# Wider loads of q, k and v, and output steps ahead of gate steps, in an attention and gated feed-forward kernel

## Chip, cores and metric

One core of one Trainium2 chip. The metric is the device time of one execution in microseconds (us). A time is the median of several executions, and each kernel was timed in turns with the kernel before on the same chip.

## The reference

Condensed:

```python
def _attn_ref(q, k, v):                      # (8, 12, 448, 64) each
    scores = np.matmul(q, k.transpose(0, 1, 3, 2)) / np.sqrt(q.shape[-1])
    attn = np.exp(scores - np.max(scores, axis=-1, keepdims=True))
    attn = attn / (np.sum(attn, axis=-1, keepdims=True) + 1e-09)
    return np.matmul(attn, v)

def _moe_ref(x, w_gate, w_val, w_out):       # x (3584, 768), d_ff 1536
    g = x @ w_gate
    return (g / (1 + np.exp(-g)) * (x @ w_val)) @ w_out
# ... x is the attention's output, heads side by side
```

## The kernel before

The 96 heads are worked in 48 pairs. One list of "visits" interleaves three score chunks of attention (matmul, then exponential) with products (sums, probabilities times values) and with steps of the feed-forward: a gate step with its value step for one block of d_ff, or an output step. GpSimd issues the loads of q, k and v, which cast from 32 to 16 bits, and it also arranges q and k for a transpose that is done by DMA. It does that for pair `pr + 3`, and loads for pair `pr + 6`, when the scores of pair `pr` begin.

```python
def load_qk16(pr, n=2):
    h0 = 2 * (pr % 2) if pr >= 14 else 0
    if h0 == 0:
        # ... a new buffer for two pairs: q16, k16 (five in turn)
    for dst, src in ((q16, q), (k16, k)):
        # ... flat: the 2 * n heads
        if pr >= SPLIT:                      # pairs from 12
            split_load(dst, h0, flat, src is q)   # two issues: partitions 0-63, 64-127
            continue
        # ...

# in each visit, after the scores:
for pr in entered:                           # pairs whose first chunk is in this visit
    if pr >= SPLIT:
        double_rest(pr)                      # GpSimd: a copy inside v
    if NPE <= pr + 3 < NPAIR:
        prep(pr + 3)                         # GpSimd: 4 copies; SyncE: DMA transpose
    if 14 <= pr + LA < NPAIR:
        load_qk16(pr + LA, 1)                # LA = 6
    if 4 <= pr // GP + 1 < NGRP:             # GP = 3
        r = pr % GP
        load_v(pr // GP + 1, 2 * r, 2 * r + 2)
# ... products ...
for pr in entered:
    for w in wq.pop(pr, []):                 # weights: {..., 6: V 3, o 0; 7: o 1}
        emit(w)
# ... blocks 2 and later; nf and no are the numbers of gate and of output steps
for y in range(nf):
    if fvq:
        run_fv()
for _ in range(no):
    run_o()
```

The softmax here doesn't subtract the row's maximum and nothing guards it: scores larger than these inputs give would overflow.

Of the kernel before, what the change touches and what calls it, by code (L numbers as in the profile page):

```python
# [11 lines left out]
FP16 = mybir.dt.float16  # L12
# [6 lines left out]
GP = 3  # L19
NPE = 11  # L20
LA = 6
RB = 5
# [3 lines left out]
SPLIT = 12  # L26
# [3 lines left out]
def kernel(  # L30
# [10 lines left out]
    nc = tc.nc  # L41
    B, H, S, D = q.shape
    DM = H * D
    DF = moe_w_gate.shape[1]
    P = 112
    NC = S // P
# [3 lines left out]
    NPAIR = B * NHP  # L50
    NGRP = NPAIR // GP
# [22 lines left out]
    raws = ctx.enter_context(tc.tile_pool(name="raws", bufs=2))  # L74
# [38 lines left out]
            nc.sync.dma_start(dst[:], src[0, 2 * pr : 2 * pr + 2].rearrange("h (p c) d -> p h (c d)", c=NC))  # L113
        raw[pr] = (rq[:], rk[:])

    pairbuf = []

    def load_qk16(pr, n=2):
        h0 = 2 * (pr % 2) if pr >= 14 else 0
        if h0 == 0:  # L120
            rows = 128 if pr >= SPLIT else P
            q16 = raws.tile([rows, 4, NC, D], FP16, tag="rq", bufs=RB, name="q16")
            k16 = raws.tile([rows, 4, NC, D], FP16, tag="rk", bufs=RB, name="k16")
            pairbuf[:] = [q16, k16]
        q16, k16 = pairbuf
        for dst, src in ((q16, q), (k16, k)):
            flat = src.rearrange("b h s d -> (b h) s d")[2 * pr : 2 * pr + 2 * n]
            if pr >= SPLIT:
                split_load(dst, h0, flat, src is q)
                continue  # L130
            nc.gpsimd.dma_start(dst[:, ds(h0, 2 * n)], flat.rearrange("h (p c) d -> p h (c d)", c=NC))
        for i in range(n):
            h = h0 + 2 * i
            raw[pr + i] = (q16[:, h : h + 2], k16[:, h : h + 2])

    def split_load(dst, h0, flat, query):
        n = flat.shape[0]
        by7 = flat.rearrange("h (r x) d -> r h x d", x=7)
        lo = (0, 3) if query else (0, 4)
        at = (0, 0) if query else (0, 1)  # L140
        for u, (x0, x1) in enumerate((lo, (lo[1], 7))):
            nc.gpsimd.dma_start(  # L142
                dst[ts(u, RS), h0 : h0 + n, at[u] : at[u] + x1 - x0, :].rearrange("p h c d -> p h (c d)"),
                by7[:, :, x0:x1, :].rearrange("r h x d -> r h (x d)"),
            )

    def load_v(g, lo=0, hi=2 * GP):
        b = g // GPB
        h0 = (g % GPB) * 2 * GP
        split = b * NHP >= SPLIT  # L150
        if lo == 0:
            v16[g] = raws.tile([128 if split else P, 2 * GP, NC, D], FP16, tag="vt", bufs=3, name="vt")
        if split:
            split_load(v16[g], lo, v[b, h0 + lo : h0 + hi], False)
            return
        nc.gpsimd.dma_start(
            v16[g][:, lo:hi],
            v[b, h0 + lo : h0 + hi].rearrange("h (p c) d -> p h (c d)", c=NC),
        )

    def double_rest(pr):
        g, r = divmod(pr, GP)
        nc.gpsimd.tensor_copy(v16[g][RS:128, 2 * r : 2 * r + 2, 0], v16[g][0:RS, 2 * r : 2 * r + 2, 0])
# [123 lines left out]
    def pv_rest(p0):  # L287
        acc = [ps_f.tile([128, 512], FP32, tag="f", name="acc") for _ in range(2)]
        for t in range(2):
            for j in range(4):  # L290
                g, r = divmod(p0 + j // 2, GP)
                for half in range(2):
                    rows = ts(half, RS)
                    nc.tensor.matmul(  # L294
                        acc[half][ts(j, 32), ds(t * H2, H2)],
                        lhsT=v16[g][rows, 2 * r + j % 2, 0, :].rearrange("p (d t) -> p t d", t=2)[:, t],
                        rhs=E[p0 + 1][rows, 3, j % 2, ds(j // 2 * H2, H2)],
                        start=(t == 0),
                        stop=False,
                    )  # L300
        return acc
# [48 lines left out]
    def scaled(p0, t, acc):  # L350
        b, hp = divmod(p0, NHP)
        kk, bb = divmod(b, NB)
        if kk not in X:
            X[kk] = xp.tile([128, NCB, NB * S], FP16, tag="X", name="X")
        nc.vector.tensor_tensor(  # L355
            X[kk][:, hp + t, ts(bb, S)], acc[:, 0:S], R[p0][:], ALU.mult
        )
# [147 lines left out]
    with tc.manual_schedule():  # L505
# [27 lines left out]
        def emit(item):  # L533
            if item[0] == "qk":
                load_qk16(*item[1:])
            elif item[0] == "V":
                load_v(item[1])
            else:
                load_w(*item)
# [4 lines left out]
        def pop_deferred(n=1):  # L544
            for _ in range(n):
                if deferred:
                    deferred.pop(0)()
# [5 lines left out]
        def add_block(i, visits):  # L553
            f1, f2, n = block(i)
            oq.extend(ffn2_wait)
            ffn2_wait.clear()
            fvq.extend([(f1, NCB * n / 2400.0)] * NFB)
            own = [(f2, NFB * OH / 2400.0)] * (2 * (n // 128))
            (oq if i == 0 else ffn2_wait).extend(own)
            count.update(visits=visits, fv=NFB, o=len(oq), at=0, more=NFB - visits)  # L560
# [8 lines left out]
        def run_o():  # L569
            gen, t = oq.pop(0)  # L570
            next(gen)
            pop_deferred(2)
            return t
# [6 lines left out]
        def left():  # L580
            return sum(2 * t for _, t in fvq) + sum(t for _, t in oq)
# [51 lines left out]
        while g < len(units) or queue:  # L633
            n = 2 if g < (WIDE - FIRST) * NC else 3
# [12 lines left out]
        def product(kind, p0):  # L647
            if kind == "sums":
                pop_deferred(99)
                deferred.extend(recips(p0, sums(p0)))  # L650
            elif kind == "both":
                pop_deferred(99)
                pv_split(p0, rests.pop(p0))
            else:
                if kind == 0:
                    pop_deferred(99)
                scaled(p0, kind, pv(p0, kind))

        def score(pr, c):
            if c == "rest":  # L660
                qk_rest(pr)
            elif pr >= SPLIT:
                qk_split(pr, c)
            else:
                qk(pr, c)
# [4 lines left out]
        for x, (chunks, todo) in enumerate(plan):  # L670
            for pr, c in chunks:
                score(pr, c)
            for _, kind, p0 in todo:
                if kind == "both":
                    rests[p0] = pv_rest(p0)
            end = min([y for y in adds if y > x] + [len(plan) + 1])
            if x == 0:
                for t in range(2):
                    scaled(p4, t, halves[t])
                add_block(0, end)  # L680
            turn2 = None
            entered = [pr for pr, c in chunks if c == 0]
            for pr in entered:
                if pr >= SPLIT:
                    double_rest(pr)
                if NPE <= pr + 3 < NPAIR:
                    prep(pr + 3)
                if 14 <= pr + LA < NPAIR:
                    load_qk16(pr + LA, 1)
                if 4 <= pr // GP + 1 < NGRP:  # L690
                    r = pr % GP
                    load_v(pr // GP + 1, 2 * r, 2 * r + 2)
            for pr, c in chunks:
                if c == 2 and pr < NPE - 2:
                    prep(pr + 2)()
            any_p = len(todo)
            if x in adds and x > 0:
                while todo:
                    product(*todo.pop(0)[1:])
                add_block(adds[x], end - x)  # L700
            while todo:
                product(*todo.pop(0)[1:])
            for pr in entered:
                for w in wq.pop(pr, []):
                    emit(w)
            tiled[0] = bool(any_p) and (not chunks or chunks[0][0] >= TILED)
            if adds[max(y for y in adds if y <= x)] < 2:
                carry = run_budget(left() / (end - x) + carry)
            else:
                at, n = count["at"], count["visits"]  # L710
                no = share(count["o"], at, n)
                nf = 1
                if no and count["more"] > 0:
                    o_left = sum(1 for y in range(at, n) if share(count["o"], y, n))
                    extra = -(-count["more"] // o_left)
                    nf += extra
                    count["more"] -= extra
                count["at"] += 1
                for y in range(nf):
                    if fvq:  # L720
                        run_fv()
                for _ in range(no):
                    run_o()
            tiled[0] = False
        run_budget(1e9)
# [35 lines left out]
```

## Time and profile before

| | kernel before |
|---|---|
| median of the first three executions | 467.22 us (466.89 to 468.92) |
| span in the profile | 464.7 us |
| TensorE busy | 446.3 us, 96% |
| GpSimd busy | 216.5 us, 47% |
| waits of TensorE that the profile names | 14 us |

The prediction below shows the lines of TensorE. Two more of the profile's page matter: GpSimd's issues of value loads (busy us, mean ns; then idle us before them and what ended most of it), and one queue of the DMA table (packets, MB, share of the 16 engines' time).

### The profile page before, as it was taken

Reading aid. Unit: us, or ns where it says so; the run is one execution under the profiler, and the core shown is the slowest. Engines: PE = TensorE matmul, PEld = TensorE weight load, DVE = VectorE, ACT = ScalarE, POOL = GpSimd, SP = SyncE. Lnnn points to the kernel's source line nnn. Section 1 sums busy time; section 2 is a strip of 40 time slices with the busy share of each in tenths; the row PEclk is TensorE's granted clock in tenths of the full one; section 3 lists DMA queues with packets and bytes.
Section 4 is the critical chain, followed back from the end, with each engine's and each line's share of the span. In section 5 each row is a group of like instructions: output and inputs, shape, how many; then the busy total and the mean of one; then the engine's idle time right before and its main releaser. Section 6 shows DMA issues by size and latency. Waiting matters only on the chain.

```text
span 464.7 us, 19305 instructions
## 1 busy us (share of the span) xinstructions
PE 446.3 (96%) x8816; PEld 256.3 (55%) x8816; DVE 238.7 (51%) x374; ACT 226.6 (49%) x335; POOL 216.5 (47%) x436
## 2 busy tenths in 40 slices
PE   8899996999999999999999999999999999999996
PEld 3355553545456666556456665555556666544564
DVE  3765752376476555646365473566347466355200
ACT  7986564635454545635454455633545542222222
POOL 8554709989989157750939328760600000000000
PEclk9999997999999999999999999999999999999999
DMA  9999997899986659853769748943332002100133
GB/s 137 199 200 202 191 177 99 117 181 125 107 101 67 75 87 135 116 54 76 103 80 115 92 65 96 157 55 76 41 66 56 16 27 60 45 1 0 35 102 103
DMA packets 88147, 44.58 MB, mean 96 GB/s; under 512 B 53121, under 2 KB 84609, under 8 KB 88065
## 3 DMA queue, kind: packets, MB, share of 16 engines
q0 software_dynamic: 48448, 23.38, 42.3%
q1 hardware_dynamic: 39376, 19.77, 23.1%
q8 instruction: 69, 1.13, 1.0%
q10 hardware_dynamic: 240, 0.20, 0.1%
q14 instruction: 14, 0.11, 0.1%
HBM read 47.19 MB, written 11.01 MB: 125 GB/s over the span
## 4 chain that ended last, share of the span: by engine, by line
PE 82%; DMA 9%; ACT 3%; issue 2%; DVE 2%; POOL 1%; ACTq 0%; SPq 0%; DVEq 0%; POOLq 0%
PE vp L407 15%; PE gp L407 15%; PE op L407 14%; PE op L404 8%; PE gp L404 6%; PE vp L404 6%; PE acc L309 5%; PE s L262 5%; PE acc L368 3%; DMA wo<-in_moe_w_out_dram 3%; DMA wg<-in_moe_w_gate_dram 2%; DMA q<-in_q_dram 2%; PE acc L294 1%; ACT E L285 1%; ACT E L253 1%
## 5 line engine op out<-in xcount | busy, mean ns | idle before, releaser
L435 DVE SCALAR_TENSOR_TENSOR t<-sg,gp 128x384 f32<-128x384 f32 (+1 forms) x96 | 58.8, 612 | 91.7 <-ACT sg L423 91.7
L269 ACT ACTIVATE E<-s 128x896 f16<-128x896 f32 x108 | 92.8, 922 | 12.4 <-PE s L262 12.2
L423 ACT ACTIVATE sg<-gp 128x384 f32<-128x384 f32 (+1 forms) x96 | 52.6, 548 | 92.7 <-PE gp L407 61.6
L407 PE MATMUL gp<-X,wg 128*32 128x384 f16 (+1 forms) x1632 | 88.6, 350 | 0.2
L407 PE MATMUL vp<-X,wv 128*32 128x384 f16 (+1 forms) x1632 | 88.0, 349 | 0.0
L468 ACT ACTIVATE osb<-op 128x384 f32<-128x384 f32 (+1 forms) x57 | 27.7, 486 | 118.1 <-PE op L407 82.2
L142 POOL DMA_DIRECT2D vt<-in_v_dram x72 | 44.0, 635 | 77.4 <-PE acc L309 75.4
L407 PE MATMUL op<-wo,hts 128*32 128x384 f16 x1728 | 77.9, 331 | 0.4 <-DVE X L355 0.4
L392 DVE RECIPROCAL R<-ssb 128x112 f32<-128x112 f32 x92 | 73.5, 829 | 0.8
L438 DVE SCALAR_TENSOR_TENSOR hts<-t,vp 128x384 f16<-128x384 f32 (+1 forms) x96 | 59.6, 621 | 11.1 <-DVE t L435 1.4
L407 PEld LDWEIGHTS <-hts 128*32 128x32 f16 x1728 | 48.8, 99 | 25.4 <-issue 2.6
L407 PEld LDWEIGHTS <-wv 128*32 128x32 f16 x1632 | 45.4, 97 | 30.5
L407 PEld LDWEIGHTS <-wg 128*32 128x32 f16 x1632 | 44.6, 97 | 26.6 <-issue 1.3
L142 POOL DMA_DIRECT2D k<-in_k_dram x70 | 42.5, 626 | 16.7 <-DMA q<-in_q_dram 7.3
L253 ACT ACTIVATE E<-s 112x896 f16<-112x896 f32 x48 | 40.3, 926 | 6.8 <-PE s L246 6.6
L142 POOL DMA_DIRECT2D q<-in_q_dram x70 | 41.7, 602 | 1.5 <-PE gp L404 0.9
L404 PE MATMUL gp<-X,wg 128*128 128x512 f16 (+1 forms) x168 | 37.7, 360 | 3.5 <-ACT E L285 3.5
L389 DVE COPY ssb<-acc 128x448 f32<-128x448 f32 x23 | 14.4, 624 | 50.6 <-PE acc L377 38.5
L404 PE MATMUL op<-wo,hts 128*128 128x384 f16 (+1 forms) x252 | 40.2, 318 | 0.0
L404 PE MATMUL vp<-X,wv 128*128 128x512 f16 (+1 forms) x168 | 37.6, 360 | 0.0
L262 PE MATMUL s<-qkT 64*32 64x448 f16 x864 | 30.6, 357 | 4.2 <-DMA qkT<-qk 4.0
L323 DVE TENSOR_TENSOR X<-acc,R 128x448 f16<-128x448 f32 x36 | 21.7, 624 | 22.3 <-PE acc L309 22.3
(60 smaller groups left out, 360.0 us busy)
## 6 DMA issues: line engine op xcount, KB each, us to landing
out_dram<-osb SPq DMA_DIRECT2D x42, 192.0 KB, 2.7
wg<-in_moe_w_gate_dram POOLq DMA_DIRECT2D x8, 288.0 KB, 11.0
wv<-in_moe_w_val_dram POOLq DMA_DIRECT2D x8, 288.0 KB, 11.4
wo<-in_moe_w_out_dram POOLq DMA_DIRECT2D x2, 1152.0 KB, 17.0
vt<-in_v_dram POOLq DMA_DIRECT2D x36, 64.0 KB, 3.4
q<-in_q_dram POOLq DMA_DIRECT2D x34, 64.0 KB, 3.7
k<-in_k_dram POOLq DMA_DIRECT2D x34, 64.0 KB, 3.5
vt<-in_v_dram POOLq DMA_DIRECT2D x36, 48.0 KB, 3.6
```

The lines of the kernel that those rows point to most:

```text
L142: nc.gpsimd.dma_start(dst[ts(u, RS), h0 : h0 + n, at[u] : at[u] + x1 - x0, :].rearrange("p h c d -> p h (c d)"), by7[:, :, x0:x1, :].rearr ...
L253: nc.scalar.activation(E[pr][:, c], s[0:P, :, 0:S], AF.Exp, scale=sm_scale)
L262: nc.tensor.matmul(s[ts(j, 32), hx, 0:S], lhsT=t[ts(hx, 64), c, ts(j, 32)], rhs=t[ts(hx, 64)].rearrange("p c q -> p (c q)")[:, S : 2 * S], ...
L269: nc.scalar.activation(E[pr][:, c], s[:, :, 0:S], AF.Exp, scale=sm_scale)
L309: nc.tensor.matmul(acc[half][ts(j, 32), ds(t * H2, H2)], lhsT=v16[g][:, 2 * r + j % 2, c + 1, :].rearrange("p (d t) -> p t d", t=2)[:, t], ...
L392: lambda i=i: nc.vector.reciprocal(rt[:, ts(i, P)], ssb[:, ts(i, P)]) for i in range(4)
L404: nc.tensor.matmul(dst, lhsT=lhsT, rhs=rhs, start=start, stop=stop)
L407: nc.tensor.matmul(dst[ts(j, 32), :], lhsT=lhsT[:, ts(j, 32)], rhs=rhs, start=start, stop=stop)
L423: nc.scalar.activation(sg[:, 0:n], gp[:, 0:n], AF.Tanh, scale=0.5)
L435: nc.vector.scalar_tensor_tensor(t1[:, 0:n], sg[:, 0:n], 1.0, gp[:, 0:n], ALU.add, ALU.mult)
L438: nc.vector.scalar_tensor_tensor(hts[:, fb, 0:n], t1[:, 0:n], 0.5 * HS, vp[:, 0:n], ALU.mult, ALU.mult)
L468: nc.scalar.activation(osb[:, ds(m0, w)], op[:, 0:w], AF.Copy, scale=1.0 / HS)
```

## The change

The intent: fewer and larger issues, so that GpSimd is less busy and loads run further ahead; and in visits without products an output step first, so that the gate step does not stand waiting for the exponentials.

```diff
     def load_qk16(pr, n=2):
-        h0 = 2 * (pr % 2) if pr >= 14 else 0
-        if h0 == 0:
-            # ... a new buffer
+        # ... a new buffer, always
...
-                if 14 <= pr + LA < NPAIR:
-                    load_qk16(pr + LA, 1)
-                if 4 <= pr // GP + 1 < NGRP:
-                    r = pr % GP
-                    load_v(pr // GP + 1, 2 * r, 2 * r + 2)
+                if pr % 2 == 0 and 14 <= pr + LA < NPAIR:
+                    load_qk16(pr + LA)
+                if pr % GP == 0 and 4 <= pr // GP + 1 < NGRP:
+                    load_v(pr // GP + 1)
...
+                for step in range(no if not any_p else 0):
+                    run_o()
                 for y in range(nf):
                     if fvq:
                         run_fv()
-                for _ in range(no):
+                for _ in range(no if any_p else 0):
                     run_o()
```

More of the change, by code (lines that the diff above doesn't have):

```diff
@@ L114, in load_qk32 @@
         raw[pr] = (rq[:], rk[:])
-    pairbuf = []
     def load_qk16(pr, n=2):
-        h0 = 2 * (pr % 2) if pr >= 14 else 0
-        if h0 == 0:
-            rows = 128 if pr >= SPLIT else P
-            q16 = raws.tile([rows, 4, NC, D], FP16, tag="rq", bufs=RB, name="q16")
-            k16 = raws.tile([rows, 4, NC, D], FP16, tag="rk", bufs=RB, name="k16")
-            pairbuf[:] = [q16, k16]
-        q16, k16 = pairbuf
+        rows = 128 if pr >= SPLIT else P
+        q16 = raws.tile([rows, 4, NC, D], FP16, tag="rq", bufs=RB, name="q16")
+        k16 = raws.tile([rows, 4, NC, D], FP16, tag="rk", bufs=RB, name="k16")
         for dst, src in ((q16, q), (k16, k)):
@@ L128, in load_qk16 @@
             if pr >= SPLIT:
-                split_load(dst, h0, flat, src is q)
+                split_load(dst, 0, flat, src is q)
                 continue
-            nc.gpsimd.dma_start(dst[:, ds(h0, 2 * n)], flat.rearrange("h (p c) d -> p h (c d)", c=NC))
+            nc.gpsimd.dma_start(dst[:, 0 : 2 * n], flat.rearrange("h (p c) d -> p h (c d)", c=NC))
         for i in range(n):
-            h = h0 + 2 * i
+            h = 2 * i
             raw[pr + i] = (q16[:, h : h + 2], k16[:, h : h + 2])
```

## The prediction

> **What bounds the kernel now.** I read the page's busy table and slices first, then TensorE's waits, then the chain that ended last around the longest wait, then timelines and the granted clock around it.
>
> ```profile
> PE 446.3 (96%) x8816; PEld 256.3 (55%) x8816; DVE 238.7 (51%) x374; ACT 226.6 (49%) x335; POOL 216.5 (47%) x436
> PEclk9999997999999999999999999999999999999999
> PE s L262 <- DMA qkT<-qk: 4.0, 1, 4.0
> PE gp L404 <- ACT E L285: 3.5, 5, 0.7
> PE s L246 <- ACT E L253: 1.4, 4, 0.4
> ```
>
> TensorE (PE) is busy for 446.3 of 464.7 us; nothing else is above 51%. Only what TensorE loses can be won. The last three lines (columns: total us, times, longest us) are its largest waits; all twelve together are 14 us. One slice of the clock line dips, the seventh (70 to 81 us), where the 4.0 us wait lies. The chain of work through that stretch (start, duration, what):
>
> ```profile
> 47.71 13.61 DMA wo<-in_moe_w_out_dram
> ...
> 61.60 0.59 POOL k L142
> 62.20 7.29 issue
> ...
> 70.09 1.18 POOL vt L142 x2
> ...
> 72.89 4.01 DMA qkT<-qk
> ```
>
> GpSimd (POOL) takes its program in order. It had issued both halves of w_out (47.7, 48.7 us), then q and k of pair 14 and q of pair 15, eight loads in all. The ninth stood until 61.60 us, just after the first w_out half landed (47.7 + 13.6 = 61.3), and the tenth until 69.50, just after the second (48.7 + 20.5 = 69.2). Earlier waits of GpSimd's loads (at 11.3, 12.5, 13.5 and 15.6 us) also name the load eight back, so I read it as at most eight of its loads in flight. Behind the two stuck k loads of pair 15 lay the copies that build pair 13's transpose. They ran at 71.3 us, the transpose left at 72.89, and TensorE needed it at 72.7.
>
> ```profile
> 72.52 0.38 PE L262 MATMUL s<-qkT 64*32 64x448 f16 x8
> 76.94 0.95 PE L262 MATMUL s<-qkT 64*32 64x448 f16 x16 [4.04 <-DMA qkT<-qk]
> 77.82 1.69 PE L368 MATMUL acc<-E,ones 112*32 112x448 f16 x16
> 79.29 5.86 PE L407 MATMUL op<-wo,hts 128*32 128x384 f16 x96
> 85.08 0.38 PE L262 MATMUL s<-qkT 64*32 64x448 f16 x8
> ...
> 78.00:79.00 1.00, 1.00 (x16) 0.41 (x12) 0.00 (x0) 1.00 (x2) 1.00 (x2) 0.50 0.14 15
> ```
>
> The last line is the second from 78 to 79 us; its third number from the end is the granted clock, 0.50. It stays at 0.5 from about 76 to 82.5 us. So the wait costs more than 4.04 us. This visit goes from 72.52 to 85.08 = 12.56 us. At the full clock its parts take 0.69 (three score chunks, 88.59 to 89.28) + 0.77 (sums, 59.97 to 60.74) + 3.90 (two output steps, 181.71 onward in the chain) = 5.36 us. **The visit loses 7.20 us**: 4.2 idle, 3.0 slow.
>
> The second loss is in visits without products:
>
> ```profile
> 226.56 0.39 PE L278 MATMUL s<-qkT 64*32 64x224 f16 x16
> 226.76 0.56 PE L262 MATMUL s<-qkT 64*32 64x448 f16 x16
> 228.03 1.46 PE L404 MATMUL gp<-X,wg 128*128 128x512 f16 x6 [0.71 <-ACT E L285]
> ```
>
> Score chunks and gate steps share three PSUM buffers. Three chunks fill them, and the gate step that follows at once must wait for the first exponential. The chunks' own pace ends at 226.56 + 0.69 = 227.25, so 0.78 us are lost. This recurs at 120.7, 174.1, 228.0, 282.2 and 336.1 us.
>
> **What the Trainium skill says.** "TensorE: Matmul & The Clock Gate", Part 1: the array falls to half its clock after an idle window of about 3.4 us and comes back after a busy one. The trace agrees in kind: 4.04 us idle, then 0.50; the recovery took some 5 us of work here. "DMA: Bandwidth & Descriptors", Queues, rings and completion order: a DMA engine alternates between queues packet by packet. The trace agrees: from 64 to 65 us the software queue moved 188 packets and the transposes 188; without transposes the software queue moved 426 packets (68 to 69 us). The same page, Rules for kernel authors: coalesce small loads. The trace shows why it is cheap for GpSimd: issues of 96 to 128 KB took 0.61 to 0.67 us (39.8 to 43.9 us), of 48 to 64 KB 0.60 to 0.64.
>
> **The change part by part.**
>
> *Loads of q, k and v.* There are 70 + 70 + 72 = 212 issues from this line. Pairs 14 to 47 keep half their q and k issues, 34 + 34 of 68 + 68, and the values keep a third, 24 of 72. That removes 116 issues of about 0.62 us, 72 us of GpSimd (216.5 to some 144). After 90 us nobody waits for GpSimd in any way that reaches TensorE, so nearly all of it is hidden. What counts is the order around 50 us. After the two w_out halves now come four wider loads (pairs 14 and 15), the copies of pair 12, two value loads, and then at once the copies of pair 13: 2 + 4 + 2 = 8 loads, so none of them is held. Copies of 13 run at about 56.0 to 57.6 us instead of 71.3 to 72.9.
>
> Their transpose then queues behind that of pair 12, whose packets end at about 66.1 us. It has about 896 packets (as many as pair 12's moved); at 188 per us it ends near 70.9 and lands near 71.5. Needed: 72.7. **The wait goes, by a slack of 1.2 us, and the slow clock with it: -7.2 us.**
>
> *The next transpose.* The wider loads of pairs 14 and 15 are now all ahead of pair 14's copies. At 66.1 us some 365 packets of w_out are left (estimate from the 66 to 68 us stretches): 68.0 at 188 per us. Then 1024 packets of q and k, 530 of them by 70.9 and the rest at 430 per us: 72.0, landed 73.6 with the 1.6 us that w_out took from last packets to landing. Copies 1.6 us (75.2), transpose 4.0 us as at 72.89, so 79.2. TensorE, no longer held, wants it at 72.52 + 5.36 + 0.4 = 78.3. **New wait +0.9 us** (0 to 2), too short to bring the clock down. Pair 15 has about 2 us of slack, pair 16 some 7.
>
> *Output steps first.* This affects blocks 2 and later, so four of the five waits (not 120.7): 4 x 0.78 = -3.1 us. The output step needs one of the other two PSUM buffers, freed before it starts (the copy out of the step before ended at 227.2), and its 1.95 us cover the exponential. But the gate step is now the last thing before the next visit, whose third chunk takes its buffer. From a 384-wide gate's start at 179.58, VectorE's read of it ended 2.53 us later; the third chunk would come at 1.94 + 0.46 = 2.40. I charge 0.2 us for each 384-wide visit and 0.05 for each 512-wide: +0.5. **Net -2.6 us.**
>
> *Sum:* -7.2 + 0.9 - 2.6 = -8.9 us. 467.2 - 8.9 = 458.3, which is 1.9% less.
>
> **Rivals.** (a) *The wait moves to pair 13 or 14.* For: the DMA engines are full from 46 to 70 us, and the transpose of pair 12 took 11.9 us from issue to landing against a median of 4.5. Against: my packet count leaves pair 13 1.2 us. If both came 2 us late, the gain would shrink to about 6: 461. A wait over 3.4 us could bring the slow clock back: 463 to 465. (b) *The transfers are hidden anyway,* and only the step order counts: -2.6, 464.6. For: GpSimd is no bound over the whole span, 47%. Against: the chain runs through its stuck queue. (c) *No new wait:* the landing lags are less than I charge, and the buffers come free in time: -10.3, 456.9, which is 2.2%. For: after 69 us the engines have room (shares 0.3 to 0.7 in places). (d) *Fewer issues free GpSimd and a new engine bounds:* nothing for it; TensorE would be 96% to 97% busy. (e) *Group loads hold GpSimd longer for a value buffer* (it stood 75.4 us in seven such waits already) and delay later copies. Against: the first load of a group already stood at the same place, and copies run three pairs ahead; 0 us.
>
> **Range and chances.** Steps (a) and (c) are 457 to 461. The 2% line is 467.22 x 0.98 = 457.9, so close under my centre that it is nearly a coin toss; I lean to the near side because of the new wait. Range 456.2 to 461.5. Faster by over 2%: 0.42; within 2%: 0.57; slower: 0.01.
>
> **What would show it.** In the changed kernel's profile: the chain no longer runs through a transpose for 4 us near 73; the clock is 1.0 from 70 to 90 us; a wait of scores for a transpose of 0 to 2 us near 78 us; the waits of gate steps for the exponential fall from five to one (the one near 120), with perhaps small waits of scores for VectorE right after these visits; GpSimd busy near 144 us. I am wrong if the eight-in-flight reading fails (the copies of pair 13 still late), if the clock dips anyway, or if a transpose under a full queue takes much longer than its packets say.

## More of the kernel before

```profile
L142 POOL DMA_DIRECT2D vt<-in_v_dram x72 | 44.0, 635 | 77.4 <-PE acc L309 75.4
q8 instruction: 69, 1.13, 1.0%
```

The second I passed over when I predicted, and it turned out to be the line that mattered: 69 packets of 16 KB are TensorE's own instructions on their way to it (shown under the result).

## The result

The changed kernel took 461.75 us in the median (461.24 to 463.44, four executions), the kernel before 467.06 (466.88 to 468.92). The ratio is 0.9884, 95% interval 0.9848 to 0.992: within 2%. A ratio here is the mean time of one kernel's fast runs over that of the other's of the same rounds, so it is not quite the ratio of the medians. The gain is 5.3 us where 8.9 were predicted, and 461.75 lies just outside the range of 456.2 to 461.5. Two more sets, on other chips, gave 461.47 and 463.02 us, ratios 0.9895 and 0.9915.

The page and TensorE's waits (total us, times, longest us) in the changed kernel; its line numbers are 6 lower, so L256 is what was L262, L401 what was L407:

```profile
PE 445.6 (97%) x8816; PEld 258.6 (56%) x8816; DVE 238.6 (52%) x374; ACT 227.1 (49%) x335; POOL 151.8 (33%) x320
PEclk9999999999999999999999999999999999999999
PE op L401 <- issue: 2.3, 4, 0.8
PE s L256 <- DMA qkT<-qk: 1.2, 1, 1.2
PE s L256 <- issue: 1.0, 1, 1.0
PE gp L398 <- ACT E L279: 0.7, 1, 0.7
PE acc L371 <- issue: 0.5, 1, 0.5
```

The 4.0 us wait is gone and the clock line has no dip. The gate step's waits went from five to one. A wait of 1.2 us for a transpose is new. But there is something that the kernel before has nowhere in this view: TensorE idle with the reason "issue", which means that it waited for nothing that the profile shows. With a further 0.2 us at a gate step, that is 4.0 us in seven waits. GpSimd fell to 151.8 us, where the prediction had 144.

GpSimd, then TensorE, around the old 4 us wait (start, duration, engine, line, operation, count, and in brackets the idle time before):

```profile
55.60 0.50 POOL L182 COPY qk<-k 128x384 f16<-128x384 f16 x1
...
61.88 0.63 POOL L136 DMA_DIRECT2D q<-in_q_dram  x1 [4.75 <-DMA wo<-in_moe_w_out_dram]
71.67 0.61 POOL L136 DMA_DIRECT2D q<-in_q_dram  x1 [9.16 <-DMA wo<-in_moe_w_out_dram]
```

```profile
72.71 0.76 PE L256 MATMUL s<-qkT 64*32 64x448 f16 x24
73.40 0.94 PE L362 MATMUL acc<-E,ones 112*32 112x448 f16 x16
74.17 1.63 PE L401 MATMUL op<-wo,hts 128*32 128x384 f16 x35
76.45 2.76 PE L401 MATMUL op<-wo,hts 128*32 128x384 f16 x61 [0.66 <-issue]
79.14 0.38 PE L256 MATMUL s<-qkT 64*32 64x448 f16 x8
...
80.92 0.38 PE L256 MATMUL s<-qkT 64*32 64x448 f16 x8 [1.20 <-DMA qkT<-qk]
```

Pair 13's copies run at 55.6 us, and the two loads that stand for the w_out halves now stand behind them, not ahead. The visit that took 12.56 us takes 79.14 - 72.71 = 6.43. But an output step is torn in two, after 35 of its matmuls, by a wait that no tile explains. It happens again later, in ordinary steps far from any dependency:

```profile
248.68 1.22 PE L401 MATMUL gp<-X,wg 128*32 128x384 f16 x24
249.65 1.22 PE L401 MATMUL vp<-X,wv 128*32 128x384 f16 x24
250.63 1.47 PE L401 MATMUL op<-wo,hts 128*32 128x384 f16 x31
252.91 0.97 PE L401 MATMUL op<-wo,hts 128*32 128x384 f16 x17 [0.81 <-issue]
```

**What these waits are.** I numbered TensorE's recorded instructions (8,816 matmuls, as many weight loads and 6 others, 17,638 in all) and set beside each such gap the last 16 KB packet of the instruction queue. A gap here runs from the start of the instruction before to the start of the one that resumes, so it holds a part that is no idle time: the seven add up to 6.2 us, of which the profile names 4.0 as idle.

```
gap, us   resumes at   instruction no.   no. mod 256   instruction packet landed   us before
0.98        76.45          2241             193              75.03                   1.42
1.33       100.97          3265             193              99.56                   1.41
0.78       246.71          9921             193             245.22                   1.49
1.14       252.91         10177             193             251.34                   1.57
0.48       256.91         10433             193             255.51                   1.40
0.59       262.56         10689             193             261.20                   1.36
0.86       290.06         11969             193             288.59                   1.47
```

All seven stop at the same place in a block of 256 instructions, and end 1.36 to 1.57 us after a packet. 1.13 MB for 17,638 instructions is 64 bytes each, so 16 KB are 256 of them. TensorE had run out of instructions. The same holds in every profile with such waits: 52 in 16 of them, all at 193, each ending 1.24 to 1.73 us after a packet landed. The Trainium skill, "Runtime: NRT & Kernel Launch", Instruction fetch mechanics, says that instructions are refilled in 16 KiB blocks of 256 over a DMA queue and calls the cost "mostly hidden". The block size agrees with the trace; the cost is not hidden here.

To see how close other blocks came, I took for each packet how late it started, counted from the moment when TensorE began the block of instructions before the one it brings, and how long before need it landed. For the 44 or 45 packets that started between 97 and 340 us:

| | late start, mean us | packets that landed under 1.7 us before need |
|---|---|---|
| kernel before | 0.41 | 1 |
| changed kernel, three profiles | 1.05, 0.89, 1.02 | 9, 6, 7 |

That the DMA engines were busy when packets came late can be read from the same traces. In the 2 us before an instruction packet started, the packets of loads, transposes and stores (they overlap, so the share can exceed 1) took 1.19, 1.30 and 1.13 of the 16 engines' time where it started over 1.5 us late (14, 12 and 14 packets of the three profiles), and 0.37, 0.28 and 0.32 where it started at most 0.5 us late (18, 21 and 18).

### The profile page after: what moved, and what is told of

It is laid out like the page before. It is cut to its first block, busy times and chain, and to the rows that moved or that the text cites. A ratio compares the mean times of both kernels' runs of the same rounds, so it can differ in the third digit from the quotient of the medians.

```text
span 461.7 us, 19197 instructions
## 1 busy us (share of the span) xinstructions
PE 445.6 (97%) x8816; PEld 258.6 (56%) x8816; DVE 238.6 (52%) x374; ACT 227.1 (49%) x335; POOL 151.8 (33%) x320
## 3 DMA queue, kind: packets, MB, share of 16 engines
q8 instruction: 69, 1.13, 1.1%
## 4 chain that ended last, share of the span: by engine, by line
PE 78%; DMA 13%; POOL 3%; issue 2%; DVE 2%; ACT 1%; ACTq 0%; POOLq 0%; DVEq 0%
PE gp L401 15%; PE vp L401 15%; PE op L401 13%; PE op L398 8%; PE gp L398 6%; PE vp L398 6%; PE acc L303 5%; PE s L256 5%; DMA wg<-in_moe_w_gate_dram 5%; DMA k<-in_k_dram 5%; PE acc L362 3%; DMA wv<-in_moe_w_val_dram 2%; PE acc L288 1%; DMA qkT<-qk 1%; PE acc L371 1%
## 5 line engine op out<-in xcount | busy, mean ns | idle before, releaser
L401 PE MATMUL gp<-X,wg 128*32 128x384 f16 (+1 forms) x1632 | 89.3, 350 | 0.4 <-issue 0.2
L401 PE MATMUL vp<-X,wv 128*32 128x384 f16 (+1 forms) x1632 | 88.8, 349 | 0.0
L401 PE MATMUL op<-wo,hts 128*32 128x384 f16 x1728 | 77.3, 326 | 2.7 <-issue 2.3
L401 PEld LDWEIGHTS <-wv 128*32 128x32 f16 x1632 | 47.4, 97 | 28.9 <-issue 0.4
L401 PEld LDWEIGHTS <-hts 128*32 128x32 f16 x1728 | 48.5, 97 | 26.6 <-issue 3.7
L401 PEld LDWEIGHTS <-wg 128*32 128x32 f16 x1632 | 45.9, 97 | 26.8 <-issue 2.9
L136 POOL DMA_DIRECT2D vt<-in_v_dram x24 | 16.0, 673 | 115.2 <-PE acc L303 115.2
L182 POOL COPY qk<-k 128x384 f16<-128x384 f16 x72 | 28.5, 396 | 28.0 <-DMA qkT<-qk 25.8
L398 PEld LDWEIGHTS <-hts 128*128 128x128 f16 x252 | 23.9, 98 | 16.0 <-issue 1.7
L256 PE MATMUL s<-qkT 64*32 64x448 f16 x864 | 30.0, 353 | 2.2 <-DMA qkT<-qk 1.2
```

The costliest lines, as they stand in the source:

```text
L182: nc.gpsimd.tensor_copy(qk7[rows, c0 : c0 + n].rearrange("p c h d -> p h c d"), src[rows, :, x0 : x0 + n])
L256: nc.tensor.matmul(s[ts(j, 32), hx, 0:S], lhsT=t[ts(hx, 64), c, ts(j, 32)], rhs=t[ts(hx, 64)].rearrange("p c q -> p (c q)")[:, S : 2 * S], ...
L398: nc.tensor.matmul(dst, lhsT=lhsT, rhs=rhs, start=start, stop=stop)
L401: nc.tensor.matmul(dst[ts(j, 32), :], lhsT=lhsT[:, ts(j, 32)], rhs=rhs, start=start, stop=stop)
```

## The experiments

**First theory:** the wide loads fill the DMA engines in bursts, instruction packets start late, and that eats what the prediction promised. **Rivals:** the fetch waits were bad luck of one profile; they come of TensorE running some 5 us earlier against the loads; the output-first order gives its gain back.

In all tables "fetch waits, late" is TensorE's idle time named "issue" from 97 to 345 us of the profile, with the number of waits, and "close" the packets that landed under 1.7 us before need, of those that started from 97 to 340 us. Both, and "late start", come from one profiled execution of each kernel; the three profiles of the changed kernel show how far such numbers scatter.

### The order alone

```diff
 # the kernel before
+                for step in range(no if not any_p else 0):
+                    run_o()
                 for y in range(nf):
...
-                for _ in range(no):
+                for _ in range(no if any_p else 0):
```

> The kernel before with the output-first order alone. Theory (the changed kernel's shortfall is instruction fetch: TensorE stood idle with reason 'issue' at seven places, each 193 instructions into a block of 256, and each wait ended about 1.4 us after a 16 KB packet of the instruction queue landed; the order itself gave 0.76 us at each of four places and nothing was given back): 3.0 us less than before, about 464.0 us; waits of gate steps for the exponential fall from 3.5 us in five to 0.7 in one; the 4.0 us wait for pair 13's transpose and the half clock stay; waits named 'issue' on TensorE under 1 us in all. Rival (the order's gain is given back by scores that wait for the gate step's buffer): 1.0 us or less, with such waits in the profile.

463.65 us beside 466.37 for the kernel before, ratio 0.9943 (0.9928 to 0.9959). Matched score by score, its trace gains 0.76 us on the trace of before at each of the four places and gives nothing back; 4 x 0.76 = 3.0. The old transpose wait stands, and no wait is named "issue":

```profile
PE s L262 <- DMA qkT<-qk: 4.2, 1, 4.2
PE gp L404 <- ACT E L285: 0.7, 1, 0.7
```

The rival is out.

### The wide loads alone, and only the first of them

```diff
 # e2: the changed kernel, old order
-                for step in range(no if not any_p else 0):
-                    run_o()
...
 # e3: besides, from pair 16 and value group 5 on as before
-                if pr % 2 == 0 and 14 <= pr + LA < NPAIR:
-                    load_qk16(pr + LA)
+                if pr + LA < 16:
+                    if pr % 2 == 0 and pr + LA >= 14:
+                        load_qk16(pr + LA)
+                elif pr + LA < NPAIR:
+                    load_qk16(pr + LA, 1)
 # ... the same for load_v: group 4 whole, later ones by thirds
```

> The changed kernel with the old order, so the wide loads alone. Theory: the parts add, so 461.75 + 3.0 = 464.8 us, 2.3 us less than before; the 4 us wait and the half clock are gone, a wait of about 1.2 us for pair 14's transpose, and waits of TensorE named 'issue' of 3 to 5 us in all. Rival (the fetch waits were bad luck of one profiled run): 462 us or less, as the waits of that run would be missing in the timed ones.

> Only the first wide loads (pairs 14 and 15 together, value group 4 whole); all later loads one pair at a time as before; old order. Theory (the later wide loads come as bursts that hold up instruction packets, and bring nothing else): 7.2 won at pair 13, 1.2 back at pair 14 and 0.7 to one fetch wait near 76 us: 5.3 us less than before, 461.8 us, 3 us faster than the wide loads throughout; at most two fetch waits after 80 us. Rival (the fetch waits come of TensorE running some 5 us earlier against the loads, or occur at random, whatever the width): the same as the wide loads throughout, 464.8 us, with as many fetch waits.

And e4 is e3 with the output-first order:

> As the run with only the first wide loads, with the output-first order: theory 461.8 - 3.0 = 458.8 us, 8.3 us less than before and 3 us less than the changed kernel; at most two fetch waits after 80 us. Rival (width does not matter): 461.8 us, as the changed kernel.

| | median us | ratio (95%) | fetch waits, late | close |
|---|---|---|---|---|
| e2, wide throughout | 464.05 | 0.9961 (0.9931 to 0.999) | 1.0 us, 3 | 5 |
| e3, first wide loads only | 463.57 | 0.9935 (0.9916 to 0.9954) | none | 2 |
| e4, e3 and order | 460.32 | 0.9868 (0.9849 to 0.9886) | 0.4 us, 1 | 2 |

e2 came out 0.7 us under what I expected, with the wait for pair 14 (1.2 us) as told, but with 2.0 us of fetch waits in all, not 3 to 5. e3 has the late fetch waits gone, as the theory says, but not the time: it lost 1.75 us at pair 14 and 1.2 at pair 15, because GpSimd spends longer on narrow issues just then and its copies come later (those of pair 15 at 79.2 us, against 76.7 in e2). So my 461.8 missed. e4 missed its 458.8 by 1.5 us. It has the same narrow issues as e3 at pairs 14 and 15, and in its profile a loss of its own besides. Two rows of the clock (stretch, its length, busy us and instructions of five engines, granted clock, DMA share, GB/s):

```profile
80.00:82.00 2.00, 0.27 (x13) 0.11 (x8) 0.00 (x0) 1.66 (x3) 2.00 (x5) 1.00 0.41 44
84.00:86.00 2.00, 2.00 (x30) 1.03 (x25) 0.00 (x0) 0.00 (x0) 1.91 (x5) 0.50 0.80 90
```

It waited 1.73 us for pair 14's transpose, some 3 us after a fetch wait of 0.82, and the clock fell to a half afterwards. The profiled execution is the slowest of the five, 461.64 us with a mean clock of 0.995; the median one, 460.32 at 0.999, cannot have lost that much to it, so the miss of 1.5 us is not the clock's; pairs 14 and 15, as in e3, are its likely place. But "too short to bring the clock down" in my prediction is not safe.

### Control, longer bursts, and an attempt to do better

```diff
 # e7: pairs 18 to 47 four at a time
+                if pr in (8, 10):
+                    load_qk16(pr + LA)
+                elif pr >= 12 and pr % 4 == 0:
+                    for p in (pr + LA, pr + LA + 2):
+                        if p < NPAIR:
+                            load_qk16(p)
 # e8: pairs 14, 15 ahead of the second half of w_out
-            7: [("o", 1)],
+            7: [("qk", 14), ("o", 1)],
 # ... and prep(pr + 3) ahead of double_rest(pr)
 # e9: e8, with narrow loads from pair 18 and group 5 on
```

> The changed kernel again, beside the others of this call. Theory: 461.5 us, 5 us less than before; 3 to 6 fetch waits of TensorE (idle with reason 'issue', ending 1.3 to 1.6 us after a 16 KB instruction packet landed), not all at the places of the first profile. Rival (those of the first profile were a fluke): 459 us and at most one.

> The changed kernel with pairs 18 to 47 loaded four pairs at a time, every fourth pair: the same bytes and packets in bursts twice as long, the first 90 us unchanged. Theory (bursts hold up instruction packets): more fetch waits after 90 us than the changed kernel, 5 to 9 us in all, and 1 to 3 us slower, about 463.5 us. Rival (what counts is the traffic, or the phase of TensorE's blocks): the same as the changed kernel within 0.7 us.

> The changed kernel with the loads of pairs 14 and 15 issued ahead of the second half of w_out, and GpSimd's copies ahead of its doubling of v. Theory: the wait for pair 14's transpose (1.2 us) goes, and that half lands some 2.3 us later, near 74 us, when the first output step that needs it is due at 74.2, so 0 to 0.5 us of a new wait there; later fetch waits as in the changed kernel: 460.7 us, 0.5 to 1.2 us less than the changed kernel. Rival (the w_out half becomes the wait): 462 us with a wait of output steps for w_out of over 1 us.

> The same, with pairs from 18 loaded one at a time and value groups from 5 by thirds, as before. Theory: the early gain of the run above and no fetch waits after 110 us: 458.5 us, the fastest. Rival (width of the later loads does not matter): equal to the run above.

| | median us | ratio (95%) | fetch waits, all | fetch waits, late | close |
|---|---|---|---|---|---|
| a1, the changed kernel | 461.47 | 0.9895 (0.9875 to 0.9914) | 3.2 us, 5 | 1.5 us, 3 | 6 |
| e7, four pairs at a time | 461.15 | 0.989 (0.9862 to 0.9917) | 2.2 us, 3 | 1.6 us, 2 | 5 |
| e8, loads ahead of w_out | 466.87 | 0.9997 (0.9959 to 1.0035) | 9.4 us, 7 | 6.3 us, 5 | 6 |
| e9, e8 and narrow later | 461.54 | 0.9891 (0.9871 to 0.9911) | 3.1 us, 3 | 0.4 us, 1 | 1 |

The control has the fetch waits again, partly at other blocks, so they are no fluke. e7 went against me: bursts twice as long are no worse. The theory of bursts was wrong in that form. e8 lost all: neither the gain nor the w_out wait that I weighed, but a wait of 1.6 us for pair 11's transpose at 64.7 us, probably because it now shares the engines with four more loads, and 9.4 us of fetch waits. Its executions spread from 463.5 to 469.3, and the profiled one is the slowest. e9 beside e8 says that narrow later loads are worth 5 us on top of the same beginning. e9 itself missed its 458.5 by 3 us: it too waits for pair 11 (1.4 us), and two fetch waits before 90 us cost it 2.7.

### The rate at which GpSimd issues

e7 made me look at what pairs two at a time and four at a time have in common: the size of one issue. A narrow issue asks for 48 or 64 KB and takes GpSimd 0.61 us, some 92 KB/us. A wide one asks for 96 or 128 KB in 0.62 us, some 180 KB/us, about what the queue was seen to move (200 GB/s, when full). **Second theory (P):** with narrow issues, GpSimd's own slowness paces the loads below what the DMA engines can move; with wide ones a queue builds up, and instruction packets share the engines with it. **Rival (B):** asking for two pairs at one visit is what delays them.

e10 keeps the changed kernel's visits and cuts the issues; e11 also goes back to the old visits; e5 and e6 make only q and k, or only the values, wide:

```diff
 # e10: from pair 20 and value group 6 on
-                    load_qk16(pr + LA)
+                    load_qk16(pr + LA, 1)
+                    load_qk16(pr + LA + 1, 1)
...
-                    load_v(pr // GP + 1)
+                    for r in range(GP):
+                        load_v(gv, 2 * r, 2 * r + 2)
```

> The changed kernel with its visits and order, the first 85 us unchanged, but from pair 20 and value group 6 on each wide issue cut into issues as small as before, one right after the other: the same bytes are asked for at the same visits. Theory P (GpSimd's 0.6 us per issue paces the loads: 48 to 64 KB per 0.61 us is some 92 KB/us, under the 200 KB/us that the queue moves, while 96 to 128 KB per 0.62 us is some 180 and fills it, so instruction packets start late): after 97 us instruction packets start 0.4 to 0.6 us late on average and at most two land within 1.7 us of need, as in the kernels with narrow loads (0.39 to 0.59; 1 to 2); 459.0 to 460.0 us, 1.5 to 2.5 us less than the changed kernel. Rival B (asking for two pairs at one visit is what delays them): late by 0.8 to 1.1 us, 5 to 9 packets within 1.7 us, as with the wide loads, and 461.5 us.

> The changed kernel with one pair at a time from pair 20 and thirds from group 6, at the visits of the kernel before. Theory P, and rival B too: the early gain as in the changed kernel (7.2 less some 2 to waits), the order's 3.0, no fetch waits after 97 us: 458.5 to 459.5 us, the fastest so far. If what differs late is not the loads: 461.5 us.

> The changed kernel with values by thirds from group 5 on (q and k wide, output first). Theory P: q and k issues of some 180 KB/us still fill the queue, two thirds of the bytes: 460.5 to 461.5 us, three or more instruction packets within 1.7 us of need after 97 us. If it is the value groups that do it: 459 to 460 us and at most two.

> The changed kernel with q and k one pair at a time from pair 16 on (values by groups, output first). Theory P: a value issue of 144 to 192 KB per 0.67 us is some 250 KB/us but there are only two in a row: 459.5 to 461 us, two to four instruction packets within 1.7 us of need after 97 us; a wait for pair 14's or 15's transpose of 1.5 to 3 us in all as with the other narrow q and k loads. If it is q and k that do it: at most two.

| | median us | ratio (95%) | fetch waits, late | late start, mean us | close |
|---|---|---|---|---|---|
| e10, small issues, same visits | 458.76 | 0.9834 (0.9811 to 0.9858) | none | 0.46 | 1 |
| e11, small issues, old visits | 459.47 | 0.9839 (0.9821 to 0.9857) | none | 0.44 | 1 |
| e5, only q and k wide | 463.35 | 0.991 (0.9888 to 0.9933) | 2.7 us, 4 | 0.95 | 6 |
| e6, only values wide | 463.71 | 0.9916 (0.9886 to 0.9947) | 0.2 us, 1 | 0.71 | 3 |

e10 is decisive between P and B: the same bytes at the same visits, only in smaller issues, and the late fetch waits are gone and with them some 3 us. What is left of the kind in its profile is the one near 76 us:

```profile
PE s L262 <- DMA qkT<-qk: 1.1, 1, 1.1
PE gp L404 <- ACT E L285: 0.7, 1, 0.7
PE op L407 <- issue: 0.6, 1, 0.6
```

How GpSimd issues after a wait for a value buffer, first the changed kernel, then e10:

```profile
238.83 1.32 POOL L136 DMA_DIRECT2D vt<-in_v_dram  x2 [8.05 <-PE acc L303]
242.03 1.25 POOL L136 DMA_DIRECT2D q<-in_q_dram  x2
243.25 1.26 POOL L136 DMA_DIRECT2D k<-in_k_dram  x2
```

```profile
237.52 3.56 POOL L142 DMA_DIRECT2D vt<-in_v_dram  x6 [5.52 <-PE acc L309]
242.96 1.19 POOL L142 DMA_DIRECT2D q<-in_q_dram  x2
244.11 1.22 POOL L142 DMA_DIRECT2D k<-in_k_dram  x2
245.28 1.24 POOL L142 DMA_DIRECT2D q<-in_q_dram  x2
246.44 1.26 POOL L142 DMA_DIRECT2D k<-in_k_dram  x2
```

The group of values is handed over in 1.3 us in one, in 3.6 in the other, and two pairs of q and k in 2.5 and 4.8. e5 and e6 were both slower than I expected. In e5's profile the fetch waits account for it, so q and k by themselves are enough to cause them. In e6's they do not: it lost 1.9 us at pair 15 (e3 lost 1.2 there), where narrow q and k made GpSimd's copies late (the transpose left at 80.6 us, landed 5.9 us later, and the scores went on at 86.57; the profile puts this wait down to an exponential that ended at the same time). And that profile, of an execution of 460.87 us, does not explain the median: four of the six took 463.7 to 465.5, three of them at a mean clock of 0.992 to 0.996, and no trace shows where. So e6's time says nothing on the values, only its row of packets does, and that from one profile: they delay some, less than q and k.

### Rate, or size of an issue?

Cutting the issues changed both. So: the size kept wide, the rate lowered by copies on GpSimd whose result nobody uses.

```diff
 # e12, e13: the changed kernel, from pair 20 and value group 6 on
         for u, (x0, x1) in enumerate((lo, (lo[1], 7))):
+            if spaced[0]:
+                nc.gpsimd.tensor_copy(scratch[1][:], scratch[0][:])   # e13: three of them
             nc.gpsimd.dma_start(
```

> The changed kernel with a copy of 128x512 on GpSimd (about 0.6 us, its result unused) ahead of each wide issue from pair 20 and value group 6 on. Size of an issue as in the changed kernel, rate halved. Theory P (rate): after 97 us instruction packets start 0.4 to 0.65 us late on average, at most two land within 1.7 us of need, and 459 to 460 us. Rival S (size of an issue): 0.8 us or more late, five or more packets within 1.7 us, 461 to 462 us.

> Control on the same chip, the changed kernel: 461.5 us, five or more instruction packets within 1.7 us of need after 97 us, under either.

> As the spaced run, with three GpSimd copies (1.7 us) ahead of each wide issue: some 50 KB/us while issuing. Theory P (rate): at most two instruction packets within 1.7 us of need after 97 us, late by 0.4 to 0.6 us on average; 459 us, unless GpSimd's copies for the transposes come late and show as waits for a transpose. Rival S (size of an issue): five or more packets within 1.7 us, 0.75 us or more late, about 460.5 us, no better than with one copy.

> Control on the same chip, the kernel with issues as small as before at the changed kernel's visits: 458.8 us and at most two packets within 1.7 us under either.

| | median us | ratio (95%) | fetch waits, late | late start, mean us | close |
|---|---|---|---|---|---|
| a2, the changed kernel, same chip as e12 | 463.02 | 0.9915 (0.9891 to 0.9938) | 2.0 us, 3 | 1.02 | 7 |
| e12, one copy ahead of each | 460.48 | 0.9859 (0.9836 to 0.9883) | 1.3 us, 3 | 0.82 | 8 |
| e13, three copies | 458.75 | 0.9825 (0.98 to 0.9851) | none | 0.30 | 1 |
| e14, e10 again, same chip as e13 | 458.9 | 0.9828 (0.9802 to 0.9854) | none | 0.38 | 1 |

With 141 us of useless work more on GpSimd (e13: 228 copies of 0.62 us), the changed kernel is 8 us faster than the kernel before, not 5. The wide issue itself does no harm if it comes seldom enough: that part of theory P holds. But e12 went against P as I had stated it. At about the same mean rate (one copy, some 90 KB/us; e10, some 92) the wide issues still started packets 0.82 us late and left eight close, as the rival on size had it, and the small ones 0.46 and one; the time, 460.48 us, lies between the two forecasts. So the rate counts, and at that rate the size counts too. A DMA engine that takes a larger share of one issue before it turns to the instruction queue would do that, but no run shows it. Nor does e13 change the rate alone: its GpSimd no longer waits for any value buffer (115.2 us of such waits in the changed kernel), so its loads also come at other moments.

## Why the prediction was wrong

In the profiled execution, matched score by score with the profile of before:

| step of the prediction | predicted us | measured us |
|---|---|---|
| pair 13's wait and the half clock | -7.2 | -7.1 (the visit took 6.43, of which 0.95 was a fetch wait) |
| new wait at pair 14 | +0.9 | +1.4 (1.20 of it shown as a wait) |
| output steps first | -3.1 + 0.5 | -3.0 + 0 |
| loads after 90 us, "nearly all of it is hidden" | 0 | +4.5 at the fetch waits (3.3 of it named as idle) |
| (no term) fetch wait at 76 us | 0 | +0.95 |
| sum | -8.9 | -3.2; the span fell by 3.0 |

That execution was the slowest of its four; the others ran 1.4 to 2.2 us faster. If the late fetch waits are all that differed, they cost those about 2 to 3 us. The traces bear that size out: from 97 to 345 us, matched in the same way, the changed kernel's three profiles lose 5.0, 2.6 and 3.1 us on that of e10.

- **Right: the eight loads in flight.** The ninth and tenth loads again stood until the w_out halves had landed, and pair 13's copies, now ahead of them, ran at 55.6 us (predicted 56.0); the packets of their transpose ended at 71.4 (predicted 70.9). A transpose has 928 packets in the trace, not 896, which moves that sum by 0.2 us.
- **Right: the half clock belonged to the wait,** and went with it. Two readings were short: the half clock lasted from 76.09 to 82.92 us, not to 82.5, so the recovery took 6.0 us from the resumption at 76.94, not 5. Not right as a rule: e4 lost the clock after a much shorter wait.
- **Right in kind: rival (a).** Pair 14's transpose was late by 1.2 us, within the 0 to 2 that I gave.
- **Wrong: the charge of 0.5 us** for scores that wait for the gate step's buffer. It never appeared, in any run with the new order.
- **The step that failed:** "After 90 us nobody waits for GpSimd in any way that reaches TensorE, so nearly all of it is hidden." I asked only who waits for GpSimd's issues to be done, and counted 72 us of them as a cost that is removed at no price. The runs showed that they were also a brake: loads late in the kernel came no faster than GpSimd issued them, and the DMA engines stayed free for TensorE's instruction packets. Taking the brake away cost about 3 us (461.5 to 463.0 us for the changed kernel; 458.8 and 458.9 with small issues at the same visits; 458.75 with wide issues slowed down). With the brake back, e10 took 458.76 us, close to the 458.3 that I had put; that is partly luck. In its profile the gain is 8.0 us, not 8.9: the wait at pair 14 and the fetch wait near 76 us cost more than I had, and the 0.5 us that never appeared make up for some of it.
- **Rival (d),** "a new engine bounds: nothing for it", was right about the engines and too narrow: what became short was TensorE's instruction supply, a queue of 1.0% of the DMA time that I had not read.
- **Rival (e):** GpSimd did stand longer for value buffers, 115.2 us against 75.4, but no wait of TensorE in that profile leads back to it.

The fastest kernel is e10 (458.76 us, ratio 0.9834), 3 us less than the changed kernel: both parts of the change, with the loads after the crowded stretch cut into issues as small as before.

## What to carry to other kernels

Before coalescing loads, ask what their slow issue was holding back: here larger issues from one engine raised the rate at which the DMA engines filled, and the packets of a small queue that TensorE depends on, its instructions, started late. When TensorE stands idle for a reason that the profile does not name, look at where in a block of 256 instructions it stopped and when the last packet of the instruction queue landed. Early in a kernel, what pays is which load stands ahead of which: here two stuck loads that moved from ahead of one pair's copies to behind them were worth 7 of the 8 us that the best kernel gained, before what later waits took back.

## What the Trainium skill lacked or had wrong

- "Runtime: NRT & Kernel Launch" (Instruction fetch mechanics) calls the cost of a 16 KiB boundary "mostly hidden". With the DMA engines busy it was an idle wait of 0.2 to 1.6 us at a time, 4.0 us in one profile of the changed kernel and 9.4 us in that of e8; TensorE resumed 1.36 to 1.57 us after the packet landed in the seven cases listed.
- "DMA: Bandwidth & Descriptors" (Rules for kernel authors) says to coalesce small transfers and names no price. Here issues of 96 to 192 KB in place of 48 to 64 KB cost some 3 us of 460 through late instruction packets, and spacing the large ones took that back (461.5 to 463.0 us against 458.75).
- "TensorE: Matmul & The Clock Gate" (Part 1) puts the fall of the clock after an idle window of about 3.4 us. e4 fell to 0.50 at 82.86 us after an idle stretch of 1.73 us (80.02 to 81.75), 3 us after another of 0.8; e6 kept its clock through one of 1.69.
- No page that I read has it: a ninth load issued by GpSimd stood until the eighth before it had landed, here for 5.7 and 7.3 us (and for 4.75 and 9.16 in the changed kernel). The traces do not tell whether the hardware or the program sets that number.
